# Cumulated logs in four 64x64 tiles, decays in two-column products, and a new placement of the stages

## The chip, the cores and the metric

One core of one Trainium2 chip. The metric is the device time of one execution in microseconds (us), median of several. "Span" is the time from the first to the last instruction in the profiled execution; it is some 2 us shorter than the device time. "Clock" is the mean clock that TensorE was granted, as a share of full speed, from the trace's first clock record on. That record comes with the first full clock, at 4.1 to 6.7 us in all traces but two that are named below; before it the dummies run at about half speed (in both kernels 128-column products start every 107 ns there, later every 56), and the mean leaves this out. An "issue" is time in which an engine waited for nothing that the profile shows. PE is TensorE, PEld its weight loads, DVE VectorE, ACT ScalarE, POOL GpSimd.

## The reference

A gated linear attention feeds a bilinear FFN. Shapes: 4 rows of the batch, 8 heads, 768 steps, head size 48; FFN 384 to 1536 to 384.

```python
state = np.zeros((B, H, D, D))
for t in range(S):
    state = alpha[:, :, t, :, None] * state + np.einsum('bhd,bhe->bhde', k[:, :, t], v[:, :, t])
    y[:, :, t] = np.einsum('bhd,bhde->bhe', q[:, :, t], state)
x = y.transpose(0, 2, 1, 3).reshape(B * S, H * D)
out = ((x @ w_a) * (x @ w_b)) @ w_out
```

## The kernel before

The 768 steps and 4 rows are cut into six chunks of two rows each; the FFN of one chunk runs on TensorE while the attention of the next is prepared. The attention works with logarithms: logs of alpha are summed in pairs of steps (`logs`), cumulated along a half chunk of 64 steps by a product with a triangular fp32 matrix (`stA`), and the exponentials of the cumulated logs scale queries and keys. The decay of the state over each half is the exponential of the sum of its logs (`decay_pe`).

```python
def logs(ch, us, eng):                       # us: which of the two rows
    ...
    nc.scalar.activation(out=x, in_=x, func=AF.Ln)
    eng.tensor_add(ch.l2[:, us]..., x[:, :, 0, :], x[:, :, 1, :])       # one instruction

def warm(n):                                 # dummy products
    w = bank("f", 4)
    for _ in range(n):
        nc.tensor.matmul(w[:, :C], lhsT=ident, rhs=ident, start=True, stop=True)

def stA(ch, u):                              # one row
    p = bank("f", 4)[:, :H * D]
    nc.tensor.matmul(p, lhsT=ut_f32, rhs=ch.l2[:, u]..., start=True, stop=True)
    ...

def decay_pe(ch):                            # u: row, r: column half of the array, g: half chunk
    for u in range(2):
        for hd in range(H):
            r, p = hd // P2, hd % P2
            for g in range(2):
                nc.tensor.matmul(s2[r * DP:r * DP + D, g, e:e + 1], lhsT=ch.l2[gs, u, hd, :], rhs=one[gs], ...)
```

Two lists say in which order the stages are issued: `START` for the first chunk with nothing beside it, `PLAN[c]` for what stands between the FFN steps of chunk c. In them "A u" is the cumulation of row u, "dec" the decay, "C u h" transposes, "D u h" scores (their masked copy `m` is made by DVE), "S u" and "Y u" the products that make y, "K u" the state's update (DVE's `tmp`), "ff i h" an FFN quarter, "warm n" n dummies. S, D, K and Y are products in 64x64 tiles.

## Time and profile before

| | kernel before |
|---|---|
| device time, first three runs | 217.27 us (216.64 to 217.68) |
| span of the profiled execution | 214.7 us |
| TensorE busy | 199.4 us, 93% |
| granted clock | 1.00 |
| ScalarE takes the first eviction of chunk 0's full-width FFN (end of the first stage) | 33.32 us |
| last TensorE result | 210.92 us |

The last two rows cut the span in two parts: 33.3 us in which the first chunk's attention is made and weights come in, and 177.6 us of FFN with attention beside it. "First part" is the moment of that eviction, "rest" the time from there to the last TensorE result. The profile's lines on where the holes are stand in the prediction.

### The profile page before, as it was taken

How to read it: one execution, taken by the hardware profiler on the slowest of the kernel's cores; microseconds unless marked ns; L12 is line 12 of the kernel's file. 1: busy time of each engine (PE TensorE's matmuls, PEld its weight loads, DVE VectorE, ACT ScalarE, POOL GpSimd, SP SyncE). 2: the span in 40 equal slices, each digit the busy share in tenths (PEclk: the TensorE clock that was granted, in tenths of full speed). 3: DMA queues.
4: the chain of work that ended last, by engine and by line, in shares of the span. 5: the costliest groups of instructions: out<-in, count | busy, mean ns of one | idle time of the engine just before them, and what ended most of it. 6: DMA issues, size and time to landing. Idle time of an engine off the chain costs nothing.

```text
span 214.7 us, 6515 instructions
## 1 busy us (share of the span) xinstructions
PE 199.4 (93%) x2826; PEld 118.5 (55%) x2826; DVE 128.4 (60%) x208; ACT 120.2 (56%) x210; POOL 54.0 (25%) x66
## 2 busy tenths in 40 slices
PE   7767897999899989999999999999999999999992
PEld 7556663556656645665545555554655545544462
DVE  4668736787736879913898918559643563045500
ACT  8853276942488997237749636876333433244421
POOL 8576839119600047000260000700100000000000
PEclk9999999999999999999999999999999999999999
DMA  6999999997999454998659538494327100320023
GB/s 162 261 257 138 228 215 219 246 254 186 324 267 280 142 101 90 261 176 184 83 147 263 119 90 86 97 275 69 62 48 151 40 0 3 92 55 0 3 58 89
DMA packets 39028, 31.24 MB, mean 145 GB/s; under 512 B 27464, under 2 KB 35160, under 8 KB 39000
## 3 DMA queue, kind: packets, MB, share of 16 engines
q0 software_dynamic: 9120, 19.27, 39.1%
q1 hardware_dynamic: 29800, 11.47, 28.0%
q8 instruction: 22, 0.36, 0.8%
q10 hardware_dynamic: 80, 0.10, 0.1%
q14 instruction: 6, 0.05, 0.1%
HBM read 25.96 MB, written 4.73 MB: 143 GB/s over the span
## 4 chain that ended last, share of the span: by engine, by line
PE 67%; DMA 11%; DVE 6%; ACT 6%; issue 3%; SPq 2%; POOL 2%; ACTq 0%; DVEq 0%
PE f L382 19%; PE f L359 17%; PE f L369 17%; DMA a_t<-in_alpha_dram 5%; PE y L309 4%; DVE m L274 3%; DMA wa_t<-in_moe_w_a_dram 3%; DMA k_t<-in_k_dram 3%; PE y L291 3%; PE f L196 3%; SPq L163 2%; PE s L273 2%; ACT L170 1%; DVE QKp L207 1%; PE s L228 1%
## 5 line engine op out<-in xcount | busy, mean ns | idle before, releaser
L359 PE MATMUL f<-xT,wa_t 128*128 128x512 bf16 (+1 forms) x240 | 59.6, 358 | 2.0 <-ACT as__745 L363 1.2
L369 PE MATMUL f<-xT,wb_t 128*128 128x512 bf16 (+1 forms) x240 | 59.7, 358 | 0.2 <-DMA wb_t<-in_moe_w_b_dram 0.2
L382 PE MATMUL f<-wo_t,prod 128*128 128x384 bf16 (+1 forms) x300 | 49.5, 320 | 0.0
L382 PEld LDWEIGHTS <-prod 128*128 128x128 bf16 x300 | 28.3, 98 | 18.0
L359 PEld LDWEIGHTS <-wa_t 128*128 128x128 bf16 x240 | 22.1, 98 | 23.8 <-issue 2.8
L369 PEld LDWEIGHTS <-wb_t 128*128 128x128 bf16 x240 | 22.6, 98 | 21.8 <-issue 1.2
L274 DVE TENSOR_TENSOR m<-s,mask 128x1024 bf16<-128x1024 f32 x22 | 26.9, 1221 | 5.7 <-PE s L273 5.4
L383 ACT ACTIVATE ot<-f 128x384 f32<-128x384 f32 (+1 forms) x25 | 12.0, 479 | 31.7 <-PE f L382 30.3
L172 POOL TENSOR_TENSOR l<-a_t 128x768 f32<-128x768 f32 x3 | 5.4, 1806 | 64.9 <-ACT a_t L170 64.9
L299 ACT ACTIVATE xT<-y 128x384 bf16<-128x384 f32 (+1 forms) x12 | 7.8, 652 | 10.3 <-DVE xT L297 5.7
L207 DVE TENSOR_TENSOR QKp<-q_t,beta 128x384 bf16<-128x384 f32 x24 | 12.9, 578 | 0.9 <-ACT beta L201 0.6
L207 DVE TENSOR_TENSOR QKp<-k_t,invb 128x384 bf16<-128x384 f32 x24 | 12.2, 552 | 0.2
L309 PE MATMUL y<-m,vx 64*64 64x128 bf16 x576 | 10.3, 218 | 2.0 <-DVE m L274 2.0
L309 PEld LDWEIGHTS <-vx 64*64 64x64 bf16 x576 | 8.9, 107 | 5.4 <-issue 5.2
L273 PE MATMUL s<-kqT 64*64 64x128 bf16 x352 | 10.5, 220 | 0.7 <-DVE kqT L252 0.7
L196 PE MATMUL f<-l,ut_f 128*128 128x384 f32 x24 | 9.2, 498 | 2.1 <-POOL l L172 1.0
L178 ACT ACTIVATE vx<-v_t 128x768 bf16<-128x768 f32 x10 | 8.0, 844 | 5.1 <-DMA v_t<-in_v_dram 5.1
L273 PEld LDWEIGHTS <-kqT 64*64 64x64 bf16 x384 | 7.6, 106 | 4.5 <-issue 2.7
L170 ACT ACTIVATE a_t<-a_t 128x1536 f32<-128x1536 f32 (+1 forms) x7 | 9.1, 1301 | 1.2 <-DMA a_t<-in_alpha_dram 1.0
L189 PE MATMUL f<-ident 128*128 128x128 bf16 x102 | 7.9, 245 | 1.4 <-POOL ident masks.py:199 1.4
L189 PEld LDWEIGHTS <-ident 128*128 128x128 bf16 x102 | 7.2, 112 | 1.5 <-POOL ident masks.py:199 1.4
L291 PE MATMUL y<-kqT,Sm 64*64 64x128 bf16 x144 | 6.1, 217 | 2.0 <-DVE tmp L341 2.0
(227 smaller groups left out, 269.0 us busy)
## 6 DMA issues: line engine op xcount, KB each, us to landing
out_dram<-ot SPq DMA_DIRECT2D x47, 96.0 KB, 2.2
a_t<-in_alpha_dram POOLq DMA_DIRECT2D x5, 768.0 KB, 8.7
k_t<-in_k_dram POOLq DMA_DIRECT2D x4, 768.0 KB, 12.5
q_t<-in_q_dram POOLq DMA_DIRECT2D x4, 768.0 KB, 8.0
v_t<-in_v_dram POOLq DMA_DIRECT2D x4, 768.0 KB, 10.5
wo_t<-in_moe_w_out_dram POOLq DMA_DIRECT2D x3, 384.0 KB, 10.5
a_t<-in_alpha_dram SPq DMA_DIRECT2D x2, 384.0 KB
k_t<-in_k_dram SPq DMA_DIRECT2D x2, 384.0 KB, 6.2
```

What stands on the lines that cost most here:

```text
L170: nc.scalar.activation(out=x, in_=x, func=AF.Ln)
L189: nc.tensor.matmul(w[:, :C], lhsT=ident, rhs=ident, start=True, stop=True)
L196: nc.tensor.matmul(p, lhsT=ut_f32, rhs=ch.l2[:, u].rearrange("p h d -> p (h d)"), start=True, stop=True)
L207: eng.tensor_mul(dst[ch.c % 2][:, u, :, i::2, :D], src[:, u, hs].rearrange("p a r d -> p r a d"), by[:, u, :, hs])
L273: nc.tensor.matmul(s2[g * HC:(g + 1) * HC, r, p, rk, :], lhsT=keysT(ch, u, 2 * h + p, g, r, rk), rhs=queriesT(ch, u, 2 * h + p, g, rs), st ...
L274: nc.vector.tensor_mul(m.rearrange("p r a k s -> p (r a) (k s)"), s2.rearrange("p r a k s -> p (r a) (k s)"), maskn(4))
L291: nc.tensor.matmul(y[rs, g, t * C:(t + 1) * C], lhsT=win(st[rs], a, t), rhs=queriesT(ch, u, a, g, rs), start=(n == 0), stop=False, skip_gr ...
L309: nc.tensor.matmul(ch.y[u][r * DP:(r + 1) * DP, g, t * C:(t + 1) * C], lhsT=win(vxs[ch.c % 2][gs, u, rk], a + P2 * r, t), rhs=ch.m[u, a // ...
L359: nc.tensor.matmul(ap, lhsT=wa_t[:, kk, f * 128:(f + 1) * 128], rhs=ff_x(ch, us)[:, kk], start=(kk == 0), stop=(kk == KT - 1))
L369: nc.tensor.matmul(bp, lhsT=wb_t[:, kk, f * 128:(f + 1) * 128], rhs=ff_x(ch, us)[:, kk], start=(kk == 0), stop=(kk == KT - 1))
L382: nc.tensor.matmul(op, lhsT=ch.prod[:, f, m * C:(m + 1) * C], rhs=wo_t[:, f, fs], start=(f == 0), stop=(f == NFF - 1))
L383: nc.scalar.activation(out=ot[:, fs], in_=op, func=AF.Copy)
```

## The change

Its intent: less TensorE time for cumulation and decay, by using all four 64x64 tiles, and a list redrawn for the new costs. The second row's logs are written with their halves exchanged, so that the two rows use four different tiles.

```diff
 def logs(ch, us, eng):
-    eng.tensor_add(ch.l2[:, us]..., x[:, :, 0, :], x[:, :, 1, :])
+    for u in range(us.start, us.stop):       # row 1: two halves, exchanged
+        for o, x in ((ALL_P, ALL_P),) if u == 0 else ((half_l(u, g), HALF[g]) for g in range(2)):
+            eng.tensor_add(ch.l2[o, u], ch.a[x, u, :, 0, :], ch.a[x, u, :, 1, :])
 def stA(ch, u):
-    nc.tensor.matmul(p, lhsT=ut_f32, rhs=ch.l2[:, u]..., start=True, stop=True)
+    for u in us:
+        for g in range(2):
+            x = half_l(u, g)
+            nc.tensor.matmul(ps_[u][HALF[g]], lhsT=ut_f32[x, x], rhs=ch.l2[x, u]..., start=True, stop=True)
 def decay_pe(ch):
             r, p = hd // P2, hd % P2
-            for g in range(2):
-                nc.tensor.matmul(s2[r * DP:r * DP + D, g, e:e + 1], lhsT=ch.l2[gs, u, hd, :], rhs=one[gs], ...)
+            nc.tensor.matmul(s2[r * DP:r * DP + D, e:e + 2 * P2 + 1:2 * P2], lhsT=ch.l2[:, u, hd, :], rhs=one[:, u:u + 2], ...)
 START = [        # the part that will matter
-    ... "warm 36", ... "K 0 V y2", "warm 8", "S 0", "mk 1 V", "D 0 1 s2", "mq 1 V", "v 1 S", "warm 12", "Y 0 VS",
-    "C 1 0 V", "C 1 1 S", "D 1 0 s2", "K 1 V y2", "ff 3 0", "ff 2 0", "S 1", "D 1 1 s2", "ff 0 0", "Y 1 VS", ...
+    ... "warm 38", ... "K 0 V y2", "S 0", "mk 1 V", "warm 14", "D 0 1 s2", "mq 1 V", "v 1 S", "Y 0 VS",
+    "C 1 0 V", "C 1 1 S", "D 1 0 s2", "ff 0 0", "ff 2 0", "K 1 V y2", "S 1", "D 1 1 s2", "Y 1 VS", ...
 PLAN = {         # all lists of chunks 0 to 5 are new (cut)
```

## The prediction

> **What bounds the kernel now.** I read the page's busy shares and its 40 slices first, then the busy time by stretches, then who waited for whom on TensorE, then the chain that ended last, and last the single records of the two groups that the change rewrites.
>
> ```profile
> PE 199.4 (93%) x2826; PEld 118.5 (55%) x2826; DVE 128.4 (60%) x208; ACT 120.2 (56%) x210; POOL 54.0 (25%) x66
> ...
> PE   7767897999899989999999999999999999999992
> ...
> DMA  6999999997999454998659538494327100320023
> ```
>
> TensorE is busy for 93% of the 214.7 us span. Its holes lie in the first twelve slices and at the very end. The stretches (PE busy is the second number) say how large they are:
>
> ```profile
> 24.00:30.00 6.00, 5.01 (x85) 4.17 (x86) 3.74 (x7) 2.43 (x7) 3.93 (x6) 1.00 1.16 234
> 30.00:36.00 6.00, 4.80 (x24) 2.15 (x22) 3.03 (x6) 4.59 (x6) 3.59 (x5) 1.00 1.15 224
> 54.00:60.00 6.00, 5.00 (x134) 3.92 (x133) 4.04 (x8) 2.89 (x6) 3.06 (x3) 1.00 1.05 314
> 78.00:84.00 6.00, 4.97 (x56) 2.59 (x55) 4.45 (x8) 4.60 (x10) 5.33 (x5) 1.00 0.43 77
> 110.00:210.00 100.00, 100.00 (x1145) 54.38 (x1137) 53.28 (x80) 49.29 (x87) 5.93 (x5) 1.00 0.41 89
> ```
>
> From 110 to 210 us there is no hole, so there only less TensorE work can help. Between 30 us (where the regular FFN loop begins) and 110 us the holes sum to 4.4 us: 1.2 in 30 to 36, 0.3 in 42 to 48, 0.4 in 48 to 54, 1.0 in 54 to 60, 0.1 in 60 to 66, 1.0 in 78 to 84, 0.4 in 100 to 110. The last 3.8 us are the output's way out and don't change. Before 30 us "busy" also counts 102 dummy matmuls (7.9 us), so what that stage is worth is the moment at which it ends, 30.0 us. The two largest waits after it:
>
> ```profile
> PE f L359 <- ACT as__745 L363: 1.2, 1, 1.2
> PE f L196 <- POOL l L172: 1.0, 1, 1.0
> ```
>
> The first is ScalarE, which loads a table and takes logs of chunk 1 while FFN results wait in PSUM. The second is a cumulation (L196) of chunk 3 that waits for POOL's 1.81 us sum of two logs. The chain in order of time gives the price, on the bounding engine, of what the change rewrites, and of a 64x64 stage beside it:
>
> ```profile
> 66.25 1.29 PE f L196 x4
> ...
> 70.79 1.09 PE s L228 x64
> ...
> 93.66 0.79 PE y L309 x48
> ```
>
> One cumulation of two rows holds TensorE for 1.29 us (0.645 per row), one decay group for 1.09 us. There are 12 rows and 4 decay groups: 7.7 + 4.4 us.
>
> [...] 384 columns in 0.645 us are 1.68 ns a column; a bf16 product of 512 columns starts every 0.215 us, 0.42 ns a column, a quarter. [...] The 48 products of L309 (64x64, 128 columns) start in fours, 3 ns apart, every 56 ns, and take 0.79 us where one after the other they would take 48 x 56 ns = 2.7 us. When 128x128 transposes give way to them at 52.1 us the first starts 0.093 us later than the stream would have had it; an FFN triple just behind such a stage has 0.75 us in the chain instead of 0.65. So a mode change costs about 0.1 us. [...] In the decay group [...] the passes of one tile start every 45 ns[...]. [...]
>
> **The change, part by part.**
> *Cumulation.* Each row becomes two 64x64 products; the second row's logs lie with halves exchanged, so that two rows fill all four tiles. [...] Two rows together should take 0.645 instead of 1.29. But the new list puts two rows together only for chunks 2 and 5. Chunks 1, 3 and 4 have FFN products or other stages between their rows, and in chunk 0 the second row's logs come about 0.8 us after the first's. So 10 x 0.645 = 6.45 in place of 7.74: -1.29 us. Between 64x64 stages (chunks 3, 4) the two free tiles can take work of the neighbour, as S and D products already interleave in the trace; estimate -0.3 us.
> *Decay.* 32 products of 64 rows (64 records, two a product) become 16 of 128 rows and two columns. Per column half of the array there are still 8 products x 2 passes x 45 ns = 0.72 us. Before, the group of the second half starts 0.21 us after the first's, while that still has passes queued, so the halves do overlap; I take 0.1 us offset each way, 0.85 us in place of 1.09: -0.25 us a group. Three of the four groups lie after 30 us: -0.75.
> *Mode changes.* I counted TensorE's order in both lists by tiling mode. After the first stage there are 66 changes before and 72 after (isolated rows of chunk 1, a decay by itself): +6 x 0.095 = +0.57 us.
> *DVE and POOL.* The second row's sum is two half-partition instructions: 0.56 us more per chunk on DVE (0.9 on POOL, half of 1.81). DVE has room after 30 us. But the first row's cumulation no longer waits for both rows' sum, and the list gives chunk 3's logs an FFN quarter more time: the 1.03 us wait at 79 us should go. -1.0.
> *Against that*, chunk 2's logs move into chunk 1's attention stage: 1.28 us table + 1.48 us logs on ScalarE in front of four FFN evictions and Y 1's eviction, with four PSUM banks to bridge it: +0.5.
> *First stage.* The extra DVE half (0.56 us) delays row 1's cumulation, then DVE's two chunk-0 products; two more dummy matmuls cost 0.1. Transposes start at 11.9 instead of 11.43 us, and DVE, busy almost without a break from 13.3 to 20 us, passes that on: +0.5. Two FFN halves now stand before K 1, so its DVE part and S 1 come later, and nothing fills TensorE beside D 1 1: +0.5. The weights come in fewer, longer packets (8 transfers for 1152 columns in place of 12 for 1024); those packets' times give the log data of chunk 1 at about 31 us, as before (31.9): 0.
> *Sum*: -1.29 -0.30 -0.75 +0.57 -1.0 +0.5 +1.0 = -1.3 us. Here I choose: a placement redrawn for the new costs should also close some of the 3.4 us of other holes after 30 us and the two that I see in the first stage. I can't place that, and give it -1.5. Together -2.8 us: 217.27 - 2.8 = 214.5.
>
> **Rivals.**
> 1. *The two passes of one fp32 product block the next tile.* Then four tiles go in sequence with half-overlap: 5 x 0.32 = 1.6 us instead of 0.645, and the decay, whose products go four in a row to one column half, would take 32 x 45 ns = 1.44 us. Against it: decay records of different tiles interleave 7 ns apart although each product's two passes are issued together. It would add about +2 x 0.95 (paired) + 6 x 0.32 (single) + 3 x 0.6 = 5.6 us to 214.5: about 220.
> 2. *The first stage decides.* If weights for FFN column 3, now in the second and longer transfer (estimated at 26 us), come late, or the chunk 1 logs come later than 32 us, ScalarE and TensorE stand in order behind them. For it: the DMA row is at 9 in all these slices. Against: the old queue has a thin place at 20 to 22 us (0.67 share) that the longer transfers fill. +1 to +3 us: 215.5 to 217.5.
> 3. *The placement does most.* All holes between 30 and 110 us go, and the first stage is not slower: -1.8 (TensorE work) -4.4 = -6: 211. For it: the holes have single causes; against: the attention stage of chunk 1 is a serial chain of DVE and TensorE, and nothing in the change makes that shorter.
>
> **Range and chances.** The work term, -1.8, is the surest (half a microsecond either way if tiles behave as in the trace); waits and first stage are -1.0 together with some 2 us either way. I take 211.7 to 217.3. 2% faster is 212.9, which needs rival 3 in good part: 0.23. 2% slower is 221.6, which needs rival 1 and more: 0.02. Within 2%: 0.75.
>
> **What would show it.** Cumulations of chunks 2 and 5: records of four tiles starting within some 20 ns, the group off TensorE in 0.65 to 0.75 us; single rows 0.65. If a pair takes over 1.2 us, the four-tile step is wrong. Decay: 32 records in 0.8 to 0.9 us; at 1.1 or more that step is wrong. PE's waits: no L196 wait of 1 us for POOL. The time at which the first full-width FFN product of chunk 0 starts: 31 against 30.0; if it is at 29 or before, my first stage is wrong, at 33 rival 2 holds. The PE busy time between that moment and 210 us should be some 1.8 us less. A new wait of over 1 us anywhere after 84 us would make the prediction wrong on the slow side.

## The result, and the profile after

| | before | after |
|---|---|---|
| device time, median of 4 runs each, same chip | 216.95 us (216.14 to 217.68) | 219.87 us (218.99 to 220.24) |
| ratio | | 1.013 (1.008 to 1.018) |
| span | 214.7 us | 218.5 us |
| clock | 1.00 | 0.983 to 0.984, in all runs |
| first part | 33.32 us | 36.68 us |
| rest, to the last TensorE result | 177.60 us | 177.97 us |

A ratio is the mean time of one kernel's fast runs over that of the other's fast runs in the same rounds, so it isn't quite the ratio of the medians that I quote. The kernel gives the right result. It is slower by 1.3%, where I had said faster by 1.3%; 219.87 lies outside my range.

Busy shares and slices of the kernel after:

```profile
PE 201.5 (92%) x2718; PEld 119.1 (55%) x2718; DVE 132.0 (60%) x220; ACT 117.7 (54%) x206; POOL 55.2 (25%) x68
...
PE   7967778999889999979999999999999999999993
...
PEclk9995899999999999999999999999999999999999
```

TensorE has 108 records of multiplications fewer (x2718 against x2826) and yet 2.1 us more busy time. The clock row has a 5 in the fourth slice: about half speed. The kernel before has none. The stretches of the kernel after, two of the prediction's and two earlier ones (PE, PEld, DVE, ACT and POOL busy, then the clock and what DMA did):

```profile
12.00:18.00 6.00, 3.94 (x104) 3.37 (x105) 3.83 (x7) 2.10 (x5) 5.11 (x9) 0.89 1.26 233
18.00:24.00 6.00, 4.67 (x100) 3.98 (x93) 3.71 (x6) 2.20 (x3) 3.90 (x5) 0.54 1.19 211
...
78.00:84.00 6.00, 5.49 (x107) 2.96 (x104) 5.80 (x11) 5.26 (x9) 3.78 (x4) 1.00 0.47 89
110.00:210.00 100.00, 99.72 (x1167) 52.89 (x1166) 55.87 (x83) 49.96 (x87) 15.56 (x15) 1.00 0.46 96
```

The same two early stretches of the kernel before:

```profile
12.00:18.00 6.00, 3.39 (x114) 2.85 (x115) 5.20 (x9) 1.61 (x2) 5.11 (x9) 1.00 1.30 229
18.00:24.00 6.00, 4.89 (x153) 3.82 (x153) 4.99 (x10) 2.91 (x5) 4.81 (x7) 1.00 1.02 143
```

From 18 to 24 us TensorE is about as busy in both, but in the kernel after it gets 100 records done where the other does 153 (not quite the same work), at a clock of 0.54. Of the later stretches, 78 to 84 us has a hole of 0.51 us where there was one of 1.03, and 110 to 210 us is as full as before. The trace's clock records say it exactly: full from 6.41 to 16.65 us, half from 16.65 to 23.48 (6.83 us), full from there.

The chain that ended last, kernel after (start, us, what): first the first stage, then one odd thing in Y 1 of chunk 1, then the stages that the change rewrote, and a transfer.

```profile
15.95 0.52 PE y L309 x12
16.47 1.41 PE f L200 x14
17.88 0.60 PE s L291 x13
18.50 1.24 DVE m L292
19.78 1.49 PE y L327 x36
...
61.84 0.56 PE y L327 x30
62.40 1.00 issue
63.40 0.47 PE y L327 x18
...
69.17 0.89 PE f L212 x8
...
73.42 1.07 PE s L246 x32
...
84.32 9.58 DMA q_t<-in_q_dram
```

In the first stage the 14 dummies of "warm 14" (L200) stand before D 0 1 (L291) and take 1.41 us of the chain; then y (L327) takes 1.49 us at half clock, where the same products take 0.89 at full clock (48 in one piece, shown further down). At 62.4 us TensorE stops for 1.00 us in the middle of the products of Y 1, and the profile names no releaser ("issue"). The pair of cumulations (L212) takes 0.89 us, the decay (L246) 1.07.

Who waits for whom on TensorE, kernel after (us in total, times, longest):

```profile
PE y L327 <- DVE m L292: 3.9, 3, 1.3
...
PE y L327 <- issue: 1.0, 1, 1.0
PE f L212 <- DVE l L183: 0.9, 2, 0.6
PE f L377 <- ACT as__734 L381: 0.8, 1, 0.8
```

The kernel before had 2.0 us in four waits for m. Its wait of the cumulation (now L212) for POOL, 1.0 us, is gone, and that for ScalarE's eviction is 0.8 in place of 1.2.

So my first question was which of three things makes the loss: the half clock, the order of the first stage, or the new features. The fourth, the gap in Y 1, I first took for a detail.

### The profile page after: what moved, and what is told of

Same layout as the page of the kernel before.

```text
span 218.5 us, 6307 instructions
## 1 busy us (share of the span) xinstructions
PE 201.5 (92%) x2718; PEld 119.1 (55%) x2718; DVE 132.0 (60%) x220; ACT 117.7 (54%) x206; POOL 55.2 (25%) x68
## 4 chain that ended last, share of the span: by engine, by line
PE 75%; DVE 7%; DMA 7%; ACT 4%; issue 4%; POOL 2%; SPq 0%; DVEq 0%; POOLq 0%
PE f L400 20%; PE f L377 18%; PE f L387 18%; DMA q_t<-in_q_dram 4%; PE y L327 4%; PE s L291 3%; PE y L309 2%; PE f L212 2%; DMA a_t<-in_alpha_dram 2%; PE s L246 2%; PE f L264 2%; DVE m L292 2%; PE f L200 2%; DVE QKp L227 1%; ACT a_t L179 1%
## 5 line engine op out<-in xcount | busy, mean ns | idle before, releaser
L400 PE MATMUL f<-wo_t,prod 128*128 128x384 bf16 (+1 forms) x300 | 50.0, 320 | 0.0
L183 POOL TENSOR_TENSOR l<-a_t 64x384 f32<-64x384 f32 (+1 forms) x9 | 9.0, 1003 | 53.7 <-ACT a_t L179 29.9
L327 PE MATMUL y<-m,vx 64*64 64x128 bf16 x576 | 11.2, 225 | 4.9 <-DVE m L292 3.9
L327 PEld LDWEIGHTS <-vx 64*64 64x64 bf16 x576 | 9.5, 112 | 8.0 <-issue 7.9
L227 DVE TENSOR_TENSOR QKp<-k_t,invb 128x384 bf16<-128x384 f32 x24 | 12.9, 579 | 1.4 <-ACT invb L221 1.3
L227 DVE TENSOR_TENSOR QKp<-q_t,beta 128x384 bf16<-128x384 f32 x24 | 12.2, 552 | 2.3 <-DMA q_t<-in_q_dram 2.3
L291 PE MATMUL s<-kqT 64*64 64x128 bf16 x352 | 10.6, 228 | 0.3 <-DVE kqT L270 0.3
L212 PE MATMUL f<-l,ut_f 64*64 64x384 f32 x48 | 9.7, 502 | 1.0 <-DVE l L183 0.9
L291 PEld LDWEIGHTS <-kqT 64*64 64x64 bf16 x384 | 7.6, 110 | 5.1 <-issue 2.5
L200 PE MATMUL f<-ident 128*128 128x128 bf16 x98 | 8.9, 271 | 1.4 <-POOL ident masks.py:199 1.4
L200 PEld LDWEIGHTS <-ident 128*128 128x128 bf16 x98 | 8.2, 124 | 1.5 <-POOL ident masks.py:199 1.4
L183 DVE TENSOR_TENSOR l<-a_t 64x384 f32<-64x384 f32 (+1 forms) x9 | 5.6, 625 | 4.7 <-ACT a_t L179 4.5
```

The lines of the kernel that those rows point to most:

```text
L183: eng.tensor_add(ch.l2[o, u], ch.a[x, u, :, 0, :], ch.a[x, u, :, 1, :])
L212: nc.tensor.matmul(ps_[u][HALF[g]], lhsT=ut_f32[x, x], rhs=ch.l2[x, u].rearrange("p h d -> p (h d)"), start=True, stop=True)
L227: eng.tensor_mul(dst[ch.c % 2][:, u, :, i::2, :D], src[:, u, hs].rearrange("p a r d -> p r a d"), by[:, u, :, hs])
L291: nc.tensor.matmul(s2[g * HC:(g + 1) * HC, r, p, rk, :], lhsT=keysT(ch, u, 2 * h + p, g, r, rk), rhs=queriesT(ch, u, 2 * h + p, g, rs), st ...
L327: nc.tensor.matmul(ch.y[u][r * DP:(r + 1) * DP, g, t * C:(t + 1) * C], lhsT=win(vxs[ch.c % 2][gs, u, rk], a + P2 * r, t), rhs=ch.m[u, a // ...
L400: nc.tensor.matmul(op, lhsT=ch.prod[:, f, m * C:(m + 1) * C], rhs=wo_t[:, f, fs], start=(f == 0), stop=(f == NFF - 1))
```

## The experiments

Eighteen kernels ran, all correct. For each: the edit, the result with the median, and the ratio to the kernel before of the same rounds. In the edits only the lines that differ are shown; "old list" is the list of the kernel before. Each call was timed on another chip, with the kernel before in the same rounds, so ratios compare across calls, times do so only roughly. A run is slow when it is over 1.5% above the fastest of the same kernel; the ranges and medians here have all runs, the ratios fast runs alone. The profiled runs of dec_inter, before_pad, dec_inter_pad and old_inter_pad were slow ones: I use their traces for where gaps lie, not for what they cost. "First part" and "rest" come from one profiled run each, and fast runs of one kernel differ by 0.5 us and more, so smaller differences of these are not shown.

### First call: features or placement, clock or order

**feat_only**: the kernel after with the old lists throughout.

```diff
-START, PLAN of the kernel after
+START, PLAN of the kernel before
```

> The new cumulations and decays with the old order of stages. Theory P (the loss is all in the new first stage; the features themselves are a small gain): 0.990 to 0.997 of the kernel before, 214.8 to 216.3 us, full clock throughout; the rows of chunks 1 to 5 stand next to each other in the old order, so each pair costs 0.99 us instead of 1.29; decays as before, 1.07 us. Theory F (the features cost more than they save: mode changes, half-partition sums on the first stage's path): 1.003 to 1.012.

Measured: 220.22 us (219.20 to 222.89), ratio 1.015 (1.011 to 1.019), clock about 1.0, first part 33.15, rest 181.29 us. The features alone make the kernel slower, with no loss in the first part. One reason shows in its chain: the sums of the logs of chunk 3 on POOL, in three pieces where there was one of 1.81 us.

```profile
79.72 1.00 POOL l L184
80.78 0.57 POOL l L184
81.35 0.50 issue
81.85 1.00 POOL l L184
```

The three take 3.1 us from start to end, and TensorE's cumulation, in the old place, waits for the halves one after the other: it lies between 80.78 and 83.68 us in place of 1.29 us. A half of 64 partitions took POOL 1.00 us here; in the kernel after halves took 0.99 to 1.00 us and whole rows 0.99 to 1.08. I had counted the two halves as 1.81 together. A part of this kernel's loss isn't the features': it also has a gap of 1.21 us in Y 1 of chunk 1, of the kind that is explained below. The features in the old lists without such a gap weren't run.

**place_only**: the new lists with the old `logs`, `stA` and `decay_pe`.

> The new order of stages with the old cumulations and decays. Theory P: at least as slow as the changed kernel, 1.012 to 1.022, with the first full-width FFN product at about 33.5 us. Theory F: close to the kernel before, 0.997 to 1.005.

Measured: 218.92 us (217.61 to 220.24), ratio 1.010 (1.006 to 1.014), first part 36.65, rest 177.13. The loss of the first part (3.3 us, half clock included) is all there without any new feature. Its runs make an experiment by themselves: three ran at clock 0.984 and took 219.49 to 220.24 us, three at 1.0 and took 217.61 to 218.34. The half clock cost about 2 us here (medians of three: 219.77 and 217.91 us), but even without it this placement doesn't win.

**old_start**: the kernel after with the first list of the kernel before.

```diff
-START of the kernel after
+START of the kernel before
```

> The changed kernel with the old list for the first stage alone. Theory P: the 3.7 us come back, ratio 0.995 to 1.002, first full-width FFN product at 30.0 to 30.8 us, granted clock 1.0 in the first 30 us. If the later stages of the new list are what is slow, 1.008 to 1.015.

Measured: 216.91 us (215.99 to 218.46), ratio 1.002 (0.998 to 1.006), clock 1.0 in the profiled run, first part 33.13, rest 177.29. The first list is the whole loss against the kernel before. But what I had predicted for the rest, some 4 us of gain, isn't there: 177.29 against 177.60.

**keep_clock**: the kernel after with dummies in the hole ahead of S 0.

```diff
-    (0, "K 0 V y2"), (0, "S 0"),
+    (0, "K 0 V y2"), (0, "warm 28"), (0, "S 0"),
```

> The changed kernel with 28 more dummy products in TensorE's 1.7 us hole before S 0, the order of all real work unchanged. Theory C (half of the loss is the granted clock, which fell to a half from 16.65 to 23.5 us): the clock stays at 1.0, the 14 dummies before D 0 1 take 0.8 instead of 1.5 us, Y 0 and the transposes behind it 0.9 and 1.1 instead of 1.5 and 1.9; the first full-width FFN product at 31.3 to 32.2 us instead of 33.7, ratio 1.000 to 1.006. Theory O (the order is all, the clock is incidental): the clock may stay up but the FFN starts at 33.3 us or later, ratio 1.010 or more.

Measured: 217.49 us (216.99 to 219.67), ratio 1.005 (1.000 to 1.009). The clock stays at 1.0 in the profiled run; one run of the six was at 0.988 and took 219.67. (A clock just under 1 alone proves no loss: in the first call the kernel before ran at 0.992 or less in seven runs, 216.09 to 216.71 us, which were no longer than its others, 216.58 to 218.09.) First part 35.12, 1.56 us less than after, rest 176.92. So the full clock in the first stage, in place of 6.83 us of half clock, was worth most of the loss (1.013 to 1.005), as expected; the other 1.8 us of the first part are the order. Its chain shows the 14 dummies of "warm 14" at full clock, on the way to DVE's m:

```profile
16.90 0.89 PE f L200 x14
...
18.19 1.23 DVE m L292
```

0.89 us here, 1.41 at half clock in the kernel after.

### Second call: crossing, decay order, first stage mended

**nocross**: old lists, new features, but the second row not exchanged (each row's two products use the two tiles of the diagonal).

```diff
-        return HALF[g if u == 0 else 1 - g]
+        return HALF[g]
```

with the sums again one instruction for both rows, and `rhs=one[:, 0:2]` in the decay.

> The features in the old order again, but the second row's logs not crossed: one sum instruction for both rows as before, both rows on the two diagonal tiles, one after the other. Theory H (the features lose in the old order because the second row's two half-partition sums come 0.55 us apart on DVE and 1.0 us apart on POOL, and TensorE stands in order behind them, as at 80.8 to 83.7 us): the loss of 1.5% shrinks to a ratio of 0.999 to 1.006, and no cumulation waits for POOL between its own products. Theory M (64x64 fp32 products and mode changes are what costs): 1.012 or more.

Measured: 219.02 us (218.86 to 219.20), ratio 1.011 (1.007 to 1.014), rest 179.43. It lies between the two expectations: 1.1% stays without the crossing. That the crossing costs the other 0.4% isn't shown: the intervals of 1.015 and 1.011 lie over each other, and the two were timed in different calls. In its chain the two rows' cumulations, both on the tiles of the diagonal, take 1.44 us a chunk in place of 1.29 (an estimate for five chunks: 0.75 us), and there is again an "issue" gap of 1.49 us in Y 1 of chunk 1.

**dec_inter**: the kernel before with two-column decays, whose products go to the two column halves of the array in turn. In the kernel after, four products of one half come ahead of four of the other, for each row.

```diff
-        for hd in range(H):
-            r, p = hd // P2, hd % P2
-            for g in range(2): ...
+        for p in range(P2):
+            for r in range(2):
+                nc.tensor.matmul(s2[r * DP:r * DP + D, e:e + 2 * P2 + 1:2 * P2], lhsT=ch.l2[:, u, r * P2 + p, :], rhs=one[:, 0:2], ...)
```

> The kernel before with the two-column decays, but the two column halves taken in turn instead of four products of one half after another. Theory D (a half takes a weight pass every 45 ns, and the next group is let in only when the last one is 5 of 8 passes on, so the order, not the number of products, sets the 1.07 us): a group holds TensorE for 0.75 to 0.9 us, ratio 0.994 to 0.999. Rival (the number of instructions or the 128-row loads set the pace): still 1.05 us or more, ratio 0.999 to 1.003.

Measured: 218.71 us (217.64 to 222.64), ratio 1.007 (1.003 to 1.011). The group itself did what it should:

```profile
105.21 0.82 PE s L229 x32
```

0.82 us in place of 1.09 and 1.07. The kernel is slower all the same, and in its trace Y 1 of chunk 1 has an "issue" gap, from 60.44 to 61.95 us. The profiled run (a slow one, 221.40 us) had half-clock windows behind that gap and behind another hole; the three runs with a clock of 0.99 or more took 217.64 to 217.92 us.

**best1**: dec_inter, and chunk 3's cumulations behind S 0 and D 0 1 of chunk 2.

```diff
-(18, 3, "A 0"), (18, 3, "A 1"), (19, 2, "S 0"), (19, 2, "D 0 1 s2"),
+(19, 2, "S 0"), (19, 2, "D 0 1 s2"), (19, 3, "A 0"), (19, 3, "A 1"),
```

> As the one with decays in turn, and chunk 3's cumulations one stage later, behind S 0 and D 0 1, so that POOL's sum is done: the 1.0 us wait of TensorE for POOL at 78 us goes. If waits on TensorE's queue count in full: 0.988 to 0.995 of the kernel before, about 214.6 us. If it only moves to chunk 3's products: 0.995 to 1.000.

Measured: 220.43 us (218.96 to 224.35), ratio 1.015 (1.011 to 1.019). A miss: S now waits for DVE's tmp up to 1.5 us (3.0 us in three waits, 2.0 in two before), an FFN product waits 0.8 us at 88.4 us until ScalarE has read a cumulation out, and the "issue" gap of 1.73 us is there again, from 58.94 to 60.67.

**start_fixed**: the kernel after with its own first list mended.

```diff
-    "K 0 V y2", "S 0", ... "warm 14", "D 0 1 s2", ... "D 1 0 s2", "ff 0 0", "ff 2 0", "K 1 V y2", "S 1", "D 1 1 s2", "Y 1 VS", "ff 3 0", "ff 0 1", "ff 1 0"
+    "K 0 V y2", "warm 28", "S 0", ... "D 0 1 s2", "warm 14", ... "D 1 0 s2", "K 1 V y2", "ff 0 0", "ff 2 0", "S 1", "D 1 1 s2", "ff 1 0", "Y 1 VS", "ff 3 0", "ff 0 1"
```

> The changed kernel with three repairs in the first stage only: 28 dummies before S 0 (keeps the clock), the 14 dummies behind D 0 1 instead of before it, K 1 ahead of the two FFN halves and one FFN half beside D 1 1. Theory P (clock plus order of the first stage is what the change loses): first full-width FFN eviction of chunk 0 at 33.2 to 34.0 us (changed kernel 36.7, kernel before 33.3), ratio 0.998 to 1.003. If the order inside the first stage is worth nothing beyond the clock: as with the dummies alone, 1.004 to 1.005.

Measured: 216.62 us (216.45 to 218.40), ratio 1.002 (0.998 to 1.006); first part 34.71 (expected 33.2 to 34.0), rest 176.17. Mending the clock and the order of its own list returns the change to the time of the kernel before, but the first part is later than I had said, and an "issue" gap in its trace fits that: TensorE stood from 21.11 to 22.58 us in the middle of K 1.

### What the gaps have in common

Several kernels with quite different lists had this gap in the same stage, and the kernel before hadn't. So I numbered TensorE's records (a bf16 product has two, its weight load and its multiplication, an fp32 product four: 24 loads and 24 multiplications for the 12 cumulations of the kernel before) in order of their start and looked at which record each gap ends, and at the packets of the instruction queue, all of 16384 bytes. The count includes the few records of TensorE's own sequencer (21 to 25 a trace). A gap is given here from the start of the last record before it to the start of the next, so the idle time is some 0.2 us less. The numbers are my count from the traces:

```
kernel          gap (us)          ends at record   last 16 KB packet starts   packet to end of gap
before          20.39 -> 21.20          706              18.73                    2.47
after           62.19 -> 63.40         1730              60.93                    2.47
feat_only       58.51 -> 59.72         1728              57.10                    2.62
old_start       58.20 -> 59.92         1728              57.38                    2.54
keep_clock      60.74 -> 61.46         1728              59.03                    2.43
nocross         58.42 -> 59.91         1730              57.27                    2.64
dec_inter       60.44 -> 61.95         1730              59.38                    2.57
best1           58.94 -> 60.67         1730              58.07                    2.60
start_fixed     21.11 -> 22.58          706              20.34                    2.24
start_fixed     59.74 -> 60.41         1730              57.66                    2.75
```

The gap doesn't belong to a stage. It belongs to a place in the program: record 1730 or 706, and 1730 - 706 = 4 x 256. (A few records are missing in a trace, so 1728 is the same place.) The restart comes 2.2 to 2.8 us behind the start of a packet in every row. (Smaller gaps, of 0.55 us, lie at record 450, again 256 before 706, in keep_clock and start_fixed, 2.9 us behind a packet.) The packets come about as often as these places: 22 on the 5674 records of the kernel before, 21 on the 5459 of the kernel after, one on some 258 and 260. That a packet holds the instructions of 256 records, and that TensorE stands in the gap for them, is my inference from place and time; no trace names a releaser. In the traces of these two kernels no boundary with 10 us and more over the 256 records ahead of it, as in FFN stretches, has an "issue" gap. With attention stages in 64x64 tiles 256 records pass in as little as 4.0 us (before, up to record 1730), and the gaps came after 5.4 us (before, record 706) and 6.3 us (after, 1730).

So the theory, "fetch" in the expectations below, became: TensorE waits at such a boundary when its packet is late, and every change in the number of TensorE instructions shifts all later stages against the boundaries. The kernel before has record 1730 in an S and D stage at 55.7 us, and the packet ahead of it came 5.9 us earlier; the kernels with the new decays, which have fewer records, have it in Y 1. place_only, with the old ones in new lists, shows no such gap.

Counted over all 20 traces, with the k-th packet given to the boundary at record 194 + 256 k: not one of 403 boundaries is passed sooner than 2.2 us after its packet starts. The packets start from 2.6 us before to 4.9 us after TensorE passes the boundary ahead. So where 256 records take less than some 7 us, TensorE can reach a boundary when the packet is not yet 2.2 us old (an estimate from these counts, 4.9 + 2.2). What makes a packet early or late within this I couldn't find out.

### Third call: moving positions by small dummies

**before_pad**, **dec_inter_pad**, **old_inter_pad** have 28 full and 64 tiny dummies (64x64 tiles, 16 columns) in place of the first 46. **old_inter** is old_start with the decay's products in turn, without the pad.

```diff
-(0, "warm 46")
+(0, "warm 28 64")
 def warm(n, tiny=0):
+    for i in range(tiny):
+        g = slice(64 * (i % 2), 64 * (i % 2) + 64)
+        nc.tensor.matmul(w[g, C:C + 16], lhsT=ident[g, g], rhs=ident[g, :16], ...)
```

> The kernel before with the first 46 dummy products replaced by 28 full ones and 64 tiny ones (64x64 tiles, 16 columns), in about the same time: nothing is changed but the number of TensorE instructions ahead of everything else (+46 products, some 92 instructions; the trace shows one 16 KB instruction packet for about every 250 TensorE records). Theory fetch: the packets are asked for at other places, one of them ahead of a dense 64x64 stage of chunk 1 (57 to 63 us) or chunk 0 (20 to 22 us), and TensorE shows an 'issue' gap of 1.2 to 1.7 us there that the kernel before hasn't: ratio 1.003 to 1.009. Rival: the gaps belong to the reordered stages, not to the fetch: no new issue gap over 0.8 us, ratio 0.998 to 1.002.

> dec_inter (kernel before with two-column decays, column halves in turn; 1.0069, issue gap 60.44 to 61.95) with the same 46 more products ahead. Its two decay groups before 60 us took away 64 products; this gives most of them back. Theory fetch: the issue gap of 1.5 us in Y 1 of chunk 1 goes or moves to a cheap place, and the decays' gain (0.82 in place of 1.09 us in three groups after the first stage) comes through: ratio 0.993 to 0.999. Rival: the loss of dec_inter belongs to the decays themselves (their results come later or their exponential waits): 1.004 to 1.010 as without the pad.

> The changed kernel with the old list of the first stage (old_start, 1.0019) and the decays' products of the two column halves in turn. Same number of instructions as old_start. Decay groups 0.82 in place of 1.07 us: -0.25 us each in three groups, ratio 0.998 to 1.000; the issue gap of 1.7 us at 58 us stays. If order within the group doesn't matter here, 1.002 as old_start.

> old_inter with the 46 more products ahead. Theory fetch: the 1.7 us issue gap at 58 us goes or becomes smaller; ratio 0.990 to 0.996, the fastest of all. If a fetch gap only moves to another dense stage: 0.997 to 1.003. Rival (gap belongs to the stage): as old_inter.

| | median us | ratio | first part | gap at a boundary |
|---|---|---|---|---|
| before_pad | 220.20 (217.17 to 220.90) | 1.009 (1.004 to 1.014) | 36.02 | 118.65 to 120.21, record 3765 |
| dec_inter_pad | 225.11 (220.58 to 226.22) | 1.024 (1.017 to 1.030) | 38.88 | 28.87 to 30.86 (962), 61.58 to 63.52 (1728) |
| old_inter | 217.08 (215.42 to 221.58) | 1.000 (0.996 to 1.004) | 33.83 | 58.64 to 60.91 (1728) |
| old_inter_pad | 217.63 (214.57 to 218.69) | 0.998 (0.993 to 1.003) | 37.64 | 28.85 to 30.54 (962) |

The pads were a bad tool: they took more time than the dummies that they replaced, and with them the clock was low in the first stage. Full clock came only at 13.70 us in dec_inter_pad and at 16.02 in old_inter_pad, and before_pad fell back to half from 7.96 to 14.79 us. (The mean clock leaves out the time before the first record, so old_inter_pad's 1.0 hides this.) Three of six runs of before_pad and two of dec_inter_pad were fast ones. As times these runs say little. Of the expectations, before_pad's ratio came in range, but not its place (there is a gap of 0.7 us at 28 us, record 962, and the one of the table); old_inter_pad's 0.998 missed its range, and dec_inter_pad refutes its own: its gap in chunk 1 didn't go. As traces they say more. In before_pad the new gap lies at 118.65 us, in chunk 3, where not one instruction differs from the kernel before, at record 3765; 194 + 14 x 256 is 3778, and by then some records are missing. In old_inter_pad the gap of 58 us is gone and one has come at record 962 = 706 + 256. In each of the four the restart is 2.6 to 2.8 us behind a packet. The clean test had to change the number of records without changing time or activity.

### Fourth call: fewer and wider dummies

I took one dummy of 512 columns for the time of 2.75 of the old ones, and this was wrong: 78 ns was the busy time of the dummies over their number, those at half clock with them. The traces show one every 216 ns against one every 56 ns at full clock, 427 against 107 at half, so a wide one takes the time of nearly four. The first stage therefore runs up to 1.3 us later in before_long (first y at 19.15 us in place of 17.91), of which 0.24 is left at the first eviction.

```diff
-(0, "warm 46") ... (0, "warm 36")
+(0, "warm 0 17") ... (0, "warm 0 13")
 def warm(n, long=0):
+    for _ in range(long):
+        nc.tensor.matmul(w.rearrange("p (r s) -> p r s", r=4), lhsT=ident, rhs=ident[repeated four times], ...)
```

**before_long** is the kernel before with this edit alone.

> The kernel before with its first 46 dummy products made 17 of four times the width and the next 36 made 13: same time, 104 TensorE records fewer, nothing else. Theory position: the boundaries at records 706, 962 and 1730 now fall inside dense 64x64 stages (1730 in Y 1 of chunk 1, where the changed kernels have it): an issue gap of 1.2 to 2 us at 57 to 60 us, ratio 1.004 to 1.012. Rival (the gaps belong to the changed stages): no new gap, 0.998 to 1.002.

Measured: 219.00 us (218.09 to 219.95), ratio 1.009 (1.004 to 1.013), clock 1.0 in all but one run (0.997). First part 33.56, as before (33.32); rest 180.13 against 177.60. Its Y 1 of chunk 1 in the chain:

```profile
57.83 0.58 PE y L311 x27
58.41 1.32 issue
59.73 0.53 PE y L311 x21
```

and the same stage in the kernel before:

```profile
57.58 0.89 PE y L309 x48
```

48 products in one piece of 0.89 us became 27 and 21 with 1.32 us between them, at record 1730, 2.69 us behind a packet that started at 57.04. In the program nothing but the number and widths of dummies over 30 us earlier is different. That is the theory's expectation in place, size and time. A second hole, of 0.8 us at 133.8 us, came with it: S waits for DVE's Sm, and Sm for 1.1 us for the transfer that brings that chunk's decay back from DRAM, issued at 129.90 us and landed at 134.18. In the kernel before the same transfer was issued at 128.10 and nothing waited; why it was late here stays open. So of the 2.5 us that the rest lost, 1.3 is the gap and some 0.8 this hole.

**old_inter_long**: old_inter with 46 dummies made 17 wide ones and 17 of the next 36 made 6, 80 records fewer. **fixed_inter_long**: start_fixed with the decay's products in turn and 126 records fewer.

> old_inter (changed kernel, old first list, column halves in turn; 1.000, issue gap of 2.3 us at record 1728) with 80 TensorE records fewer ahead (46 dummies made 17 wide ones, 17 of the 36 made 6). Theory position: record 1730 now lies in an FFN stretch behind Y 1; the 2.3 us gap goes, and no other of over 1 us before 110 us: ratio 0.988 to 0.995, that is 214 to 215.5 us, where the prediction had put the changed kernel. Rival: gap stays in Y 1 (then at another record), ratio 0.998 to 1.003.

> The changed kernel with its own first stage mended (start_fixed, 1.0017; issue gaps 1.46 at record 706 and 0.68 at 1730), column halves in turn, and 126 records fewer ahead. Theory position: both gaps go; with the decays' 0.25 us each this gives 0.985 to 0.993. Rival: as start_fixed less the decays, 0.997 to 1.001.

Measured: old_inter_long 213.89 us (213.41 to 214.92), ratio 0.986 (0.982 to 0.990), rest 175.55; no gap at any boundary. fixed_inter_long 214.95 us (214.77 to 216.47), ratio 0.992 (0.988 to 0.996), rest 175.51; one gap of 0.70 us is left at record 706. Both are faster than the kernel before. old_inter, which has the same lists and features, stood at 1.000, with a gap of 2.3 us at record 1728. But not all of the 1.4% between them is position: old_inter's clock was 0.977 to 0.999 in its six runs against 0.991 to 1.0, its trace has half clock right behind the gap (62.12 to 65.54 us) and once in the first stage (17.75 to 21.16), and the dummies take other times.

### Fifth call: how the loss and the gain divide

**after_long**: the kernel after, its lists and features as they are, with 46, 38 and 14 dummies made 17, 14 and 5 wide ones. **old_start_long**: old_inter_long with the decay in the change's own order. **dec_inter_long**: dec_inter with 46 dummies made 17 wide ones and 3 of the 36 made 1.

> The changed kernel as it is, its dummies made fewer and wider in the same time (46 to 17, 38 to 14, 14 to 5), 124 records fewer. Its hole before S 0 stays, so the clock drop of 3.4 to 6.8 us in the first stage should stay, and the first stage's order too. Theory position and clock: the 1.2 us gap in Y 1 of chunk 1 goes, the rest of the loss stays: first full-width FFN product near 33.7 us as in the changed kernel, ratio 1.003 to 1.009 in place of 1.013. If wider dummies also keep the clock at 1.0, the first stage is some 2 us shorter: 0.993 to 1.000. Rival: 1.013 as the changed kernel.

> old_inter_long with the decay's products in the change's own order (old_start with the dummies of old_inter_long). Decay 1.07 us again. Theory: three groups of 0.25 us after the first stage: 0.3 to 0.4% above old_inter_long, 0.989 to 0.992 (old_inter_long, other rounds: 0.986). If the order of the decay's products is worth nothing: 0.984 to 0.988.

> dec_inter (the kernel before with two-column decays, column halves in turn; 1.007 with an issue gap of 1.5 us at record 1730) with 62 records fewer (46 dummies to 17 wide ones, 3 of the 36 to 1), which puts record 1730 behind Y 1. Theory: the gap goes, three groups of 0.27 us come through: 0.994 to 0.999. Rival (the decays' two columns cost something else): 1.003 to 1.009.

| | median us | ratio | first part | rest |
|---|---|---|---|---|
| after_long | 217.59 (217.06 to 218.34) | 1.001 (0.998 to 1.005) | 35.78 | 176.15 |
| old_start_long | 214.48 (214.26 to 214.70) | 0.987 (0.984 to 0.990) | 33.00 | 175.98 |
| dec_inter_long | 215.63 (215.33 to 216.94) | 0.993 (0.990 to 0.997) | 32.63 | 177.04 |

after_long, slices of the clock: the 5 is gone.

```profile
PEclk9999999999999999999999999999999999999999
```

Wide dummies instead of narrow ones turn the change's 1.013 into 1.001: the clock stays up (in the profiled run; two of the six were at 0.988 to 0.989 and took 217.91 and 218.34), and no gap is left at a boundary. dec_inter likewise goes from 1.007 to 0.993: by this its gap, with the half clock behind it, made it slow, and not its decays (the dummies changed too). In old_start_long the change's features and later lists stand beside the old first list with a good position, and give 214.48 us. What still separates after_long from it is the first list alone: 2.8 us in the first part, 3.1 us in the medians. The chain of old_start_long, in the stage whose counterpart is shown above:

```profile
17.40 1.15 DVE m L295
18.58 0.89 PE y L330 x48
...
25.38 0.89 PE y L330 x48
```

and of after_long:

```profile
17.26 1.19 PE f L202 x5
18.85 1.24 DVE m L294
20.13 0.89 PE y L329 x48
...
25.42 0.41 PE y L311 x8
26.23 1.24 DVE m L294
27.50 0.89 PE y L329 x48
```

DVE's masked scores come at 18.85 in place of 17.40, because five wide dummies, 1.19 us, stand ahead of the scores; the delay is 1.55 us at the first y and 2.12 us at the second, where S 1 (L311) has just waited for K 1's DVE part, which the list puts behind two FFN halves.

The decay's order can't be told from the times: old_inter_long at 0.986 and old_start_long at 0.987 were timed in different calls, and their intervals lie over each other. In the profiles, 1.07 against 0.82 us a group is sure, the rest (175.98 against 175.55) agrees with it.

old_inter_long, at 213.89 us, beats both kernels; old_start_long at 214.48 does so with the least scatter.

### Half clock: what sets it off

The changes of the clock records are whole multiples of 3.41 us apart (in the kernel after 10.24, 6.83 and 194.56 us: 3, 2 and 57 times). I added up TensorE's busy time in each full-clock window of 3.41 us in all 20 traces (from 2 to 208 us). All eight windows with 1.06 to 1.59 us were followed by half clock, among them the one of the kernel after (13.24 to 16.65 us: 1.38 us) and of place_only (1.35). Of four windows with 1.60 to 1.74 us two were. Of the windows above that one was, with 2.45 us: before_pad's, full of tiny products. The kernel before has its lowest window at 1.74 and kept its clock. This is counted, not tested one by one; but keep_clock, which filled the hole, and after_long, whose lowest window in the first stage had 1.90 us, kept it in their profiled runs. No sharp limit comes out (1.60 us kept the clock, 1.69 and 1.73 did not), and one kernel can do either: place_only kept its clock in three of six runs. That it matters where the windows fall is my guess. None of the eight windows was idle: each had 1.06 us or more of work in its 3.41.

## Why the prediction was wrong

Two steps failed. The first is the first stage: I gave it +1.0 us, with "two more dummy matmuls cost 0.1" in it, and the first part came out 3.36 us later: 1.80 by the order of the list, 1.56 by the half clock, which was no term of my sum. The second is the rest, to which I gave -3.8: without a gap it is shorter by only 1.45 us (after_long), because the three steps that made up most of it (placement -1.5, cumulation -1.29, decay -0.75) gave a fraction of it, and in the kernel as measured a gap at a record boundary in Y 1, with what followed it, took 1.82 us back. Features and later lists without these losses (old_start_long) took 214.48 us, where I had predicted 214.5 for the whole; that is luck: its rest gained 1.62 us and not 3.8, and its first part lost nothing where I had +1.0. The parts of the 3.73 us (last TensorE result 214.65 against 210.92), from the "first part" and "rest" of single profiled runs:

| | predicted | measured |
|---|---|---|
| first part: order of the list (35.12 - 33.32, keep_clock) | +1.0 | +1.80 |
| first part: half clock (36.68 - 35.12, keep_clock) | not in the sum | +1.56 |
| rest, with a good position (176.15 - 177.60, after_long) | -3.8 | -1.45 |
| rest, position and what follows it (177.97 - 176.15) | not in the sum | +1.82 |
| sum | -2.8 | +3.73 |

The division between order and clock depends on the pair of kernels. With after_long (first part 35.78) it would be 2.46 and 0.90, but that kernel's five wide dummies take 1.19 us of the chain where keep_clock's 14 take 0.89, so part of its 2.46 is not the change's order. place_only's runs, at two clocks, lay some 2 us apart. Within the -1.45, place_only (rest 177.13, no gap in Y 1) gives -0.5 for the lists, which leaves -1.0 for the features in them: an estimate from one profile each.

*Cumulation, -1.29: failed in size.* Four tiles do work together, as step and view said: in the pair of chunk 2 the first records of the four tiles start within 0.11 us. But the pair holds TensorE for 0.89 us in the chain, 0.99 with the changes of mode around it, against 1.29: -0.3 instead of -0.65. (In chunk 5 the pair took 0.80.) And a single row, for which I had 0.645 as before (an estimate), took 0.79 us in chunk 1 where both its halves were ready. The other row of chunk 1 took 1.28, because its half sums come one after the other and its two products start 0.49 us apart. The rows of chunks 3 and 4 run among other stages and can't be priced. So the step gained about nothing in sum (an estimate from these figures).

*Decay, -0.75: failed.* "I take 0.1 us offset each way, 0.85 us": it took 1.07. I had seen that the second half's group starts 0.21 us behind the first's, and took it for an offset that is paid once or twice. It is paid by every group: four products (8 passes, 45 ns apart, with 128 rows as before with 64) go to one half, and the next four, for the other half, are let in 0.21 us later, when 5 of the 8 are through. Four such groups are 3 x 0.21 + 8 x 0.045 = 0.99 us (an estimate from these records), and 1.07 was measured. In turn (dec_inter) a group took 0.82. So the step's size was right for another order of products than the change has.

*DVE and POOL: right on the wait, wrong on the cost.* The 1 us wait of the cumulation for POOL went, as said. On DVE a half took 0.55 us in the kernel after and a whole row 0.56 in both (once 1.19), as I had assumed for the 0.56. But a half row took POOL 0.99 us, where I had 0.9, so the sums take 3.1 us instead of the 2.7 I had, and in an old list (feat_only) this opens a wait of its own.

*Chunk 2's logs and the rest: a new wait after 84 us*, which I had named as what would make the prediction wrong: at 95.0 us TensorE stands 1.2 us for m, behind QKp, behind the q of chunk 3, which is issued later in the new list and lands at 93.92 us. The new lists also have a wait of 0.8 us at 57.6 us, K 1 for ScalarE's eviction of Y 0, that the kernel before hasn't.

*First stage, +1.0: mis-sized, its dummies the worst.* I wrote "two more dummy matmuls cost 0.1". I had counted dummies and not looked where they stand: behind D 0 1 in the old list, where TensorE has time, ahead of it in the new, on the chain to DVE's m. That is 0.89 us at full clock (keep_clock) and 1.41 at half (after). The term that I did give +0.5, the extra DVE half, was nearly absorbed: S 0 starts at 15.95 us, in the kernel before at 15.82. The third term, K 1 behind two FFN halves, was right (+0.5; 0.6 by the two chains above).

*The placement, -1.5, that I said I couldn't place:* there was no ground for it. With a good position the rest is shorter by 1.45 us (after_long) to 1.6 us (old_start_long) with all features in it, so the lists alone can hardly have given half of the 1.5 (by the estimate above). The mode changes I had counted rightly (66 and 72, the traces confirm it); what the six more cost no run measures by itself.

*Not in the sum at all:* the clock and the gaps at record boundaries. The clock was in reach: the old list's "warm 8" fills just that hole, the change drops it, and I read the dummies only as busy time that counts for nothing. The gaps were in reach only as a question: the page of the kernel before lists 16 KB packets of an instruction queue, and its list of waits has one "issue" of 0.6 us; I read neither.

*The rivals.* Rival 1 (passes block the next tile) is refuted: pairs at 0.89 us, not 1.6. But what it said of the decay was right in kind: four products in a row to one column half do cost, though 1.07 us and not 1.44. Rival 2 (the first stage decides) had the right place, and nearly the size that came, +1 to +3 us, but by the wrong cause: the weights were there (the second, longer transfer by 27.1 us), and it was order and clock. Its sign came: the first full-width FFN product started at 33.72 us, where I had 31. Rival 3 is refuted. My chances gave 0.02 to slower by over 2%, and it wasn't; within 2% held. The range failed because I spread it for errors of the terms, and not for terms that I hadn't thought of.

One caution on the 214.48: the kernel before itself stands 0.6 us at record 706, and what that costs wasn't measured. No run moves the kernel before to a position without a gap (before_long moved it to a worse one), and none tests wide dummies on it without a gap. So how much of the 0.986 to 0.993 is the change, and how much position and dummies, stays open. Against dec_inter_long (0.993, same rounds), which has the old lists and cumulation, decays in turn and another position, old_start_long is 0.6% faster, with the decay in the slower order; what is left of position in this I can't tell.

## What to carry to other kernels

Number TensorE's records and know where every 256th falls. In this kernel, dense in small tiles, the gaps without a releaser, 0.7 to 2.3 us, lay at such boundaries (records 706, 962, 1730), and an edit of dummies alone brought one of 1.32 us (before_long). Test an edit at two or three positions (wider dummies move them, but took 216 ns for 56 here, so choose their number by the pace in the trace) before judging it at the level of one per cent. When a list changes, look at what stands ahead of each product on the chain to another engine, dummies too (14 of them cost 0.89 to 1.41 us here), and look for stretches of 3.41 us that lose half their TensorE work: all eight with 1.06 to 1.59 us of work were followed by half clock here. It is worth trying products of the two column halves in turn: here it made a group of 16 decays 0.82 us in place of 1.07.
